# The first block's first product in plain float32, its weights in three loads, seven warm-ups

## The chip, the cores and the metric

The kernel runs on one core of a Trainium2 chip. The metric is the device time of one execution in microseconds; the median of three runs is given. A core has engines that run side by side and wait for each other through semaphores: TensorE (PE in the profile, its weight loads PEld) multiplies matrices, VectorE (DVE), ScalarE (ACT) and GpSimd (POOL) work on tiles, and SyncE (SP) starts most of the DMA transfers.

## The reference, cut to what matters

Two branches are computed from `q` (2048 x 512) and mixed by a gate per row. Branch `a` is a short causal convolution of `k` with four taps, times `v`, then a causal convolution as long as the sequence (by Fourier transforms), plus a direct term, times `q`. Branch `b` is a two-layer network on `q`.

```python
g = sigmoid((x * gate_w).sum(-1, keepdims=True))
k_shift = sum(k_pad[:, t:t + S, :] * shift_k[:, ks - 1 - t] for t in range(ks))
kv = k_shift * v
y = irfft(rfft(kv, 2 * S) * rfft(ssm_k, 2 * S))[:S] + kv * ssm_D
a = q * y
b = relu(x @ w1) @ w2          # x: 2048 x 512, w1: 512 x 1792, w2: 1792 x 512
out = g * a + (1 - g) * b
```

The change touches the first numbers of `x @ w1`, and the load of the taps `shift_k`.

## The kernel before, in words

**Products in three.** Both layers of branch `b` are computed almost to float32 from operands that are rounded to a shorter format (float32r). An operand is split into a rounded part `h` and the rest `l`: `split` (L288 to L302) has ACT (or DVE) copy the loaded tile into `h`, and DVE subtracts `h` from the tile to give `l`. A product of a weight block and a tile of `x` is then three matmuls added in PSUM: `h` by `h`, `h` by `l`, `l` by `h`.

**Tiles.** `x` transposed comes as four chunks of 512 rows of the sequence, each in four slices `k` of 128 along the 512 channels; such a slice is a tile of 128 x 512, 256 KB. `w1` gives 14 blocks `f` of 128 output columns. A block of the first layer for one chunk is thus four slices of three matmuls, 12 in all, into one bank of PSUM. The 14 blocks are worked in two halves (`ERAS`), and within each half chunk after chunk: first layer, then second layer.

**The first block of work.** For the first chunk the blocks f = 0 to 3 (`G` = 4) are done together, slice by slice, so that work can begin with the first slice of everything. Their weights come slice-wise in tiles of 128 x 512 (`wf`). `mlp1_first` writes the order out by hand: for slice 0 first `h`-`h` and `h`-`l` of blocks 0 and 1, then of blocks 2 and 3, then `l`-`h` of all four; for slices 1 to 3 each of the three terms for all four blocks. That is 12 matmuls a slice, 48 in all, on line L362.

**Its loads.** The weights of slice 0 are loaded by ACT's queue in two halves of 256 columns (L329), each followed by ACT's rounding copy of that half (L334), and DVE's rest of the whole tile (L337). The other slices of weights and all of `x` are loaded by SP's queue in the order x0, x1, w1, x2, w2, x3, w3 (L288); ACT rounds them at L299, except x0, which DVE rounds; DVE takes the rests at L302.

**Warm-ups.** Before all that PE does nine matmuls on a constant tile (`warm`, L753, `WARM` = 9).

**The planner.** Operations are not issued as written but as `Plan.order` decides: a simulation with costs written by hand (`MM` = 0.227 for a matmul, `TILES` = 0.865 for a visit of small tiled matmuls, `ISSUE` = 0.47 for starting a DMA, `DMA_RATE`), ranks, buffers that must be free, and lists that hold an order (`fifo`). The three lists `turnACT`, `turnDVE` and `turnPE` fix the order of the first block's work on these engines. A matmul planned before `PE_COLD` = 4.4 counts twice its cost. The result is one fixed order per engine. The rest of the work, the convolutions among it, is fitted in by rank: stage 1 of the Fourier transforms (L459) and the later stages (L575, L652, L727) are plain float32 matmuls in tiles of 32 or 64 rows and columns.

**The taps.** `conv_x(0)` loads the four rows of taps, repeated over the 128 partitions, in two loads of two rows each from SP's queue (L497), 512 KB written by each. DVE multiplies by them at L512 and L515.

Of the kernel before, what the change touches and what calls it, by code (L numbers as in the profile page):

```python
# [13 lines left out]
S, D, DFF = 2048, 512, 1792  # L14
P = 128
# [51 lines left out]
def _flat(r):  # L67
    for x in r if isinstance(r, tuple) else (r,):
        yield from _flat(x) if isinstance(x, tuple) else (x,)


class Plan:
# [5 lines left out]
    def add(self, eng, dur, rank, fn, deps=(), take=(), give=(), dma=0, fifo=(), tiles=False, port=False, alt=None, pair=0, soon=False, ends=False):  # L78
        rank = tuple(_flat(rank))
        op = dict(tiles=tiles, alt=alt, port=port or eng == "POOL" and not dma, eng=eng, dur=dur, rank=rank, fn=fn, take=tuple(take), give=tuple(give), dma=dma, fifo=tuple(fifo),  # L80
                  pair=pair, soon=soon, ends=ends or soon, wait=0, next=[], asked=0.0, n=len(self.ops), rest=(), member=False)
        op["fn"] = fn if alt is None else lambda: fn(op["eng"])
        for d in deps:
            if d is not None:
                d["next"].append(op)
                op["wait"] += 1
        for q in fifo:
            self.turn.setdefault(q, []).append(op["n"])
        self.ops.append(op)
        return op  # L90
# [144 lines left out]
def act_time(n, psum=False):  # L235
    return n * 0.000833 + (0.05 if psum else 0.093)


def dve_time(n):
    return n * 0.001042 + 0.12  # L240


MM = 0.227
TILES = 0.865
SWITCH = 0.19
ROW = P * D * 4


def build(tc, wf, xp, qn, kn, vn, hn, dn, sh, gw, w1, w2, cs1, ccf, cci, cib, out):
    nc = tc.nc  # L250
# [6 lines left out]
    mp = pool("mp")  # L257
# [11 lines left out]
    add = plan.add  # L269
    T = {}  # L270
    cpool = [None, None]

    def tile_of(key, tag, w=D, dt=F32, bufs=None, rows=P, p=None):
        nm = tag + "_" + "_".join(map(str, key[1:] if len(key) > 1 else key))
        T[key] = (p or cpool[0]).tile([rows, w], dt, tag=tag, bufs=bufs or room.get(tag, 1), name=nm)
        return T[key]

    def bank(key, tag="cv"):
        T[key] = pm.tile([P, D], F32, tag=tag, bufs=room0[tag], name="_".join(map(str, key)))
        return T[key]  # L280

    room0 = dict(room)
    rows = lambda x: x.rearrange("p (r d) -> p r d", d=D)
    mm = nc.tensor.matmul


    def loaded(key, src, rank, p=None, tag="raw", deps=(), eng="SP"):
        go = lambda: (nc.sync if eng == "SP" else nc.scalar).dma_start(tile_of(key, tag, p=p), src)  # L288
        return add(eng, ISSUE, rank, go, deps, take=[tag], dma=ROW, fifo=[tag])

    xdone, wdone, xhigh = {}, {}, {}
    ERAS = [range(0, NF // 2), range(NF // 2, NF)]
    CHUNKS = [list(range(NCHUNK)), list(range(NCHUNK))[::-1]]

# [11 lines left out]

    def load_x(era, c, k, rank):
        key = ("x", era, c, k)
        ld = loaded(key, xp[c, k], rank - 3, mp)
        xhigh[era, c, k], xdone[era, c, k] = split(key, "x", (0, rank), ld, 4, mp, ["x"], ["raw"], "DVE" if rank == -1000 else "ACT", rank < -900)  # L310

    def load_w(i, f, rank):
# [4 lines left out]
    def load_first(k, rank):  # L317
        key = ("w", 0, "g", k)
        if k:
            ld = loaded(key, wf[k], rank, tag="ev")  # L320
            wdone["gh", k], wdone["g", k] = split(key, "w0", -2000, ld, WB, wp, ["w1"], ["ev"], "ACT", True)
            return
        hi, lo = ("w", "h", 0, "g", 0), ("w", "l", 0, "g", 0)
        z = [slice(0, 2 * P), slice(2 * P, D)]

        def ld(i):
            if not i:
                tile_of(key, "ev")
            nc.scalar.dma_start(T[key][:, z[i]], wf[0][:, z[i]])  # L329

        def h(i):
            if not i:
                tile_of(hi, "w0h", dt=F32R, bufs=WB, p=wp)
            nc.scalar.copy(T[hi][:, z[i]], T[key][:, z[i]])  # L334

        def l():
            nc.vector.tensor_tensor(tile_of(lo, "w0l", dt=F32R, bufs=WB, p=wp), T[key], T[hi].bitcast(F32), op=OP.subtract)  # L337

        for i in range(2):
            e = add("ACT", ISSUE, -3000 + i, lambda i=i: ld(i), (), [] if i else ["ev"], dma=ROW // 2, fifo=[] if i else ["ev"])  # L340
            f = ["w1", "turnACT"] if not i else ["turnACT"]
            wdone["gh", 0, i] = add("ACT", act_time(D // 2), -2000, lambda i=i: h(i), [e] if not i else [e, wdone["gh", 0, 0]], f[:-1], fifo=f)
        wdone["g", 0] = add("DVE", dve_time(D), -2000, l, [wdone["gh", 0, 1]], (), ["ev"], port=True, fifo=["turnDVE"])

    def part(h, f, k):
        if f < G:
# [7 lines left out]
    def mlp1_first():  # L354
        prev = [None] * G
        terms = (("h", "h"), ("h", "l"), ("l", "h"))
        first = [(0, n, f) for m in range(2) for n in range(2) for f in (2 * m, 2 * m + 1)] + [(0, 2, f) for f in range(G)]
        for i, (k, n, f) in enumerate(first + [(k, n, f) for k in range(1, 4) for n in range(3) for f in range(G)]):
            def go(k=k, f=f, n=n):
                a, b = terms[n]  # L360
                ps = bank(("m1", 0, 0, f), "cv") if k == n == 0 else T["m1", 0, 0, f]
                mm(ps, part(a, f, k), T["x", b, 0, 0, k], start=k == n == 0, stop=k == 3 and n == 2)  # L362

            prev[f] = add("PE", MM, (1, -9, i), go, [((wdone["gh", k] if k else wdone["gh", 0, f // 2]), xhigh[0, 0, k]), (xdone[0, 0, k],), (wdone["g", k],)][n] + (prev[f],),
                          ["cv"] if k == n == 0 else (), fifo=["turnPE"])
        for f in range(G):
            mlp1_out(0, 0, f, prev[f])
# [121 lines left out]
    sload = [None]  # L489

    def conv_x(c):
        rank = (1, X0 + XP * c)
        if c == 0:
            def taps():
                tile_of(("sht",), "sht", 4 * D)
                for j in (2, 0):
                    nc.sync.dma_start(rows(T["sht",])[:, j:j + 2], sh[j:j + 2].partition_broadcast(P))  # L497

            sload[0] = add("SP", 2 * ISSUE, rank[1] - 3, taps, dma=4 * ROW)
        for m in range(c + 2 if c else 0, c + 3):  # L500
            kload[m] = load_in(("k", m), kn[:, 2 * m:2 * m + 2], rank[1])
        vload[c] = load_in(("v", c), vn[:, R * c:R * c + R], rank[1])
        w = lambda j, n: rows(T["sht",])[:, j:j + 1].to_broadcast([P, n, D])
        prev = None
        for j in (3, 2, 1, 0):
            dst = ("acc", c) if j == 3 else ("tmp", c, j)
            tag = dst[0]

            def mul(j=j, dst=dst, part=None):
                o = T[dst] if part == 1 else tile_of(dst, dst[0], R * D)  # L510
                if part is None:
                    nc.vector.tensor_tensor(rows(o), rows(T["k", c + (j == 1)]), w(j, 2), op=OP.mult)  # L512
                else:
                    z, u = slice(part * D, (part + 1) * D), slice((1 - part) * D, (2 - part) * D)
                    nc.vector.tensor_tensor(o[:, z], T["k", c + (j == 0) + part][:, u], T["sht",][:, j * D:(j + 1) * D], op=OP.mult)  # L515

            def plus(dst=dst):
                nc.vector.tensor_tensor(T["acc", c], T["acc", c], T[dst], op=OP.add)  # L518

            if j % 2:  # L520
                e = add("DVE", dve_time(R * D), rank, mul, [kload[c + (j == 1)], sload[0]], [tag], fifo=[tag], port=True)
            else:
                e = add("DVE", dve_time(D), rank, lambda f=mul: f(part=0), [kload[c + (j == 0)], sload[0]], [tag], fifo=[tag], port=True)
                e = add("DVE", dve_time(D), rank, lambda f=mul: f(part=1), [kload[c + (j == 0) + 1], e], port=True)
            if j != 3:
                e = add("DVE", dve_time(R * D), rank, plus, [e, prev], (), ["tmp"] + (["in"] if j == 0 else []), port=True)
            prev = e
        e = add("DVE", dve_time(R * D), rank, lambda: nc.vector.tensor_tensor(T["acc", c], T["acc", c], T["v", c], op=OP.mult),
                [prev, vload[c]], (), ["in"], port=True)
        return ("x", ("acc", c), e, ["acc"], rank)  # L530
# [218 lines left out]
    def warm():  # L749
        ps = bank(("warm",))  # L750
        one = nc.const_aps.tensor(1.0, (P, D), mybir.dt.bfloat16)
        for _ in range(WARM):
            mm(ps, one[:, :P], one, start=True, stop=True)  # L753

    w = add("PE", WARM * 2 * MM / 2, (-3,), warm, (), ["cv"], ["cv"])
    for k in range(4):
# [61 lines left out]
PATIENCE = 0.5  # L818
BEHIND = 2
G = 4  # L820
WARM = 9
DMA_AHEAD = 2.0
DMA_RATE = 300000.0
DMA_LAG = [0.575, 0.8]
# [4 lines left out]
ISSUE = 0.47  # L829
# [61 lines left out]
```

## Time and profile before

| | before |
|---|---|
| median of three runs (lowest to highest) | 385.71 us (385.69 to 385.95) |
| the profiled execution's own time | 385.97 us |
| its span, first to last instruction | 384.2 us |
| granted TensorE clock, mean | 0.999 |
| PE busy / weight loads | 379.8 us / 273.8 us |
| DVE / ACT / POOL busy | 266.7 / 128.8 / 91.5 us |
| moved by DMA | 92.51 MB, 241 GB/s |

In a row of the timeline the first number is the start in microseconds of the span, the second how long the row lasts (several instructions of one kind are merged, with their count behind an x), then engine, line, operation and tiles, and in brackets how long the engine was idle before and what ended that. A q behind an engine's name means its sequencer, which also starts DMAs. In a list of waits a row gives who waited for whom, the microseconds in total, how many times, and the longest. A row of stretches gives for each engine its busy microseconds and its instructions, then the granted clock, the mean busy share of the 16 DMA engines and the GB/s moved. A row of DMA issues gives the queue, the count, the size and the median microseconds from issue to landing. Durations of matmul rows overlap: the next can stream while the one before drains, so the pace is read from the starts.

### The profile page before, as it was taken

To read this page: it belongs to the slowest core of one execution; us is meant where nothing else is said; L and a number is where in the kernel's file an instruction comes from. 1 tells how busy PE (TensorE), PEld (TensorE's weight loads), DVE (VectorE), ACT (ScalarE), POOL (GpSimd) and SP (SyncE) were. 2 spreads that over 40 slices of the span, in tenths; PEclk is the share of its full clock that TensorE was granted. 3 is DMA by queue.
4 is the path that set the end of the run, shared out by engine and by line. 5 is a ranking of instruction groups with operands and counts; after the bars stand their busy time and mean duration, and the time that the engine had idled before them with its cause. 6 is when DMAs were issued, how large, how long until landed. Compare 5 with 4: busy or idle time off the path is not lost.

```text
span 384.2 us, 6567 instructions
## 1 busy us (share of the span) xinstructions
PE 379.8 (99%) x2505; PEld 273.8 (71%) x2505; DVE 266.7 (69%) x356; ACT 128.8 (34%) x242; POOL 91.5 (24%) x77
## 2 busy tenths in 40 slices
PE   9999999999999999999999999999999999999996
PEld 5888788668877788788655765565587788688684
DVE  4698999797989028114799687897872347687691
ACT  5643524573147525533224022313400333012100
POOL 0000000000000000000199968866995001000000
PEclk9999999999999999999999999999999999999999
DMA  7997893898648763589867876686460798399331
GB/s 274 368 317 255 298 351 113 293 333 323 208 121 330 295 234 109 185 296 275 285 203 238 307 265 227 241 308 232 139 204 3 241 342 320 120 325 357 117 124 56
DMA packets 43474, 92.51 MB, mean 241 GB/s; under 512 B 4625, under 2 KB 7201, under 8 KB 43442
## 3 DMA queue, kind: packets, MB, share of 16 engines
q1 hardware_dynamic: 43090, 91.77, 68.8%
q8 instruction: 20, 0.33, 0.4%
q10 hardware_dynamic: 288, 0.26, 0.2%
q14 instruction: 12, 0.10, 0.1%
q0 software_dynamic: 64, 0.05, 0.0%
HBM read 61.66 MB, written 30.41 MB: 240 GB/s over the span
## 4 chain that ended last, share of the span: by engine, by line
PE 99%; DVE 0%; DVEq 0%; issue 0%
PE m L406 14%; PE m L407 13%; PE m L408 13%; PE m L376 13%; PE m L377 12%; PE m L378 12%; PE iv L652 4%; PE f_h L575 4%; PE f_x L575 4%; PE m L362 3%; PE s1x L459 2%; PE s1h L459 2%; PE cy L727 2%; PE warm L753 1%; DVE o L677 0%; DVEq L887 0%
## 5 line engine op out<-in xcount | busy, mean ns | idle before, releaser
L623 POOL TENSOR_TENSOR p<-p,ha 128x512 f32<-128x512 f32 x32 | 41.1, 1308 | 202.2 <-DVE ha L617 201.6
L406 PE MATMUL m<-w1h_h,hh 128*128 128x512 f32 x224 | 88.7, 396 | 0.0
L407 PE MATMUL m<-w1l_l,hh 128*128 128x512 f32 x224 | 87.3, 390 | 0.0
L408 PE MATMUL m<-w1h_h,hl 128*128 128x512 f32 x224 | 87.2, 389 | 0.0
L389 ACT ACTIVATE hh<-m 128x512 fp32r<-128x512 f32 x56 | 33.1, 598 | 126.4 <-PE m L378 122.1
L392 DVE SCALAR_TENSOR_TENSOR hl<-m,hh 128x512 fp32r<-128x512 f32 x56 | 38.3, 688 | 44.5 <-ACT hh L389 44.3
L376 PE MATMUL m<-xh_h,w0h_h 128*128 128x512 f32 x160 | 63.0, 394 | 0.0
L377 PE MATMUL m<-xl_l,w0h_h 128*128 128x512 f32 x160 | 62.3, 390 | 0.0
L378 PE MATMUL m<-xh_h,w0l_l 128*128 128x512 f32 x160 | 62.3, 389 | 0.0
L406 PEld LDWEIGHTS m<-w1h_h,hh 128*128 128x128 f32 x224 | 42.0, 188 | 19.1 <-ACT ev L464 6.5
L408 PEld LDWEIGHTS m<-w1h_h,hl 128*128 128x128 f32 x224 | 42.0, 188 | 9.0
L407 PEld LDWEIGHTS m<-w1l_l,hh 128*128 128x128 f32 x224 | 42.1, 188 | 8.3
L376 PEld LDWEIGHTS m<-xh_h,w0h_h 128*128 128x128 f32 x160 | 30.0, 188 | 11.1 <-issue 4.2
L378 PEld LDWEIGHTS m<-xh_h,w0l_l 128*128 128x128 f32 x160 | 30.0, 188 | 6.4
L377 PEld LDWEIGHTS m<-xl_l,w0h_h 128*128 128x128 f32 x160 | 30.0, 188 | 6.0
L518 DVE TENSOR_TENSOR acc<-acc,tmp 128x1024 f32<-128x1024 f32 x24 | 29.3, 1222 | 0.6
L302 DVE TENSOR_TENSOR w1l_l<-raw,w1h_h 128x512 fp32r<-128x512 f32 x14 | 9.4, 686 | 17.7 <-ACT w1h_h L299 17.7
L662 ACT COPY bv<-iv 128x512 f32<-128x512 f32 x16 | 8.7, 589 | 37.1 <-PE iv L652 31.9
L515 DVE TENSOR_TENSOR tmp<-in,sht_sht 128x512 f32<-128x512 f32 x32 | 20.8, 685 | 0.1
L623 POOL TENSOR_TENSOR p<-p,qa 128x512 f32<-128x512 f32 x16 | 20.7, 1317 | 0.0
L617 DVE TENSOR_TENSOR ha<-f_x,ha 128x1024 f32<-128x1024 f32 x16 | 19.5, 1221 | 1.3 <-DVE qb L617 0.5
L623 POOL TENSOR_TENSOR p<-p,qb 128x512 f32<-128x512 f32 x16 | 20.3, 1290 | 0.0
(72 smaller groups left out, 468.1 us busy)
## 6 DMA issues: line engine op xcount, KB each, us to landing
sa<-ev SPq DMA_DIRECT2D x64, 256.0 KB, 3.0
sb<-bv SPq DMA_DIRECT2D x32, 256.0 KB, 3.4
br<-sb SPq DMA_DIRECT2D x16, 512.0 KB, 6.8
raw<-xp SPq DMA_DIRECT2D x28, 256.0 KB, 4.2
raw<-w SPq DMA_DIRECT2D x24, 256.0 KB, 3.8
r_x<-sa SPq DMA_DIRECT2D x12, 512.0 KB, 5.1
in<-kn SPq DMA_DIRECT2D x10, 512.0 KB, 5.0
r_h<-sa SPq DMA_DIRECT2D x10, 512.0 KB, 6.3
```

The lines of the kernel that those rows point to most:

```text
L376: mm(ps, part("h", f, k), T["x", "h", xe, c, k], start=k == 0, stop=False)
L377: mm(ps, part("h", f, k), T["x", "l", xe, c, k], start=False, stop=False)
L378: mm(ps, part("l", f, k), T["x", "h", xe, c, k], start=False, stop=k == 3)
L389: nc.scalar.activation(tile_of(("hh", era, c, f), "hh", dt=F32R, p=mp, bufs=HB), T["m1", era, c, f], AF.Relu)
L392: nc.vector.scalar_tensor_tensor(tile_of(("hl", era, c, f), "hl", dt=F32R, p=mp, bufs=HB), T["m1", era, c, f], 0.0, T["hh", era, c, f].bit ...
L406: mm(ps, T["hh", era, c, f][:, z], T["w", "h", 1, f], start=f == fs[0], stop=False)
L407: mm(ps, T["hh", era, c, f][:, z], T["w", "l", 1, f], start=False, stop=False)
L408: mm(ps, T["hl", era, c, f][:, z], T["w", "h", 1, f], start=False, stop=f == fs[-1])
L515: nc.vector.tensor_tensor(o[:, z], T["k", c + (j == 0) + part][:, u], T["sht",][:, j * D:(j + 1) * D], op=OP.mult)
L518: nc.vector.tensor_tensor(T["acc", c], T["acc", c], T[dst], op=OP.add)
L575: mm(ps[b][32 * j:32 * j + 32, :], T[k("cf")][at, 64 * j + 32 * o:64 * j + 32 * o + 32], T[k("r", t, j // 2)][at, (j % 2) * D:(j % 2 + 1) ...
L623: nc.gpsimd.tensor_tensor(planes("p", dst, n), planes("p", dst, n), planes(src, u, n), op=OP.add if sign > 0 else OP.subtract)
```

## The change

- Block 0 of slice 0 is no longer three matmuls of split operands. It is one matmul in plain float32, straight from the loaded tiles of weights and `x`; the matmuls that come after it in slice 0 are those of blocks 1, 2 and 3, nine in all.
- The first weights come in three loads, of 128, 128 and 256 columns, with a rounding copy for each. The plain product waits for the first load (`wdone["load", 0]`) and for the load of x0 (`xload`). The whole tile is still rounded and its rest taken; later chunks use it.
- The taps come in one load of four rows.
- `WARM` is 7 and not 9.

```diff
-    xdone, wdone, xhigh = {}, {}, {}
+    xdone, wdone, xhigh, xload = {}, {}, {}, {}
...
-        ld = loaded(key, xp[c, k], rank - 3, mp)
+        ld = xload[era, c, k] = loaded(key, xp[c, k], rank - 3, mp)
...
-        z = [slice(0, 2 * P), slice(2 * P, D)]
+        z = [slice(0, P), slice(P, 2 * P), slice(2 * P, D)]
...
-        for i in range(2):
-            e = add("ACT", ISSUE, -3000 + i, lambda i=i: ld(i), (), [] if i else ["ev"], dma=ROW // 2, fifo=[] if i else ["ev"])
+        for i in range(3):
+            e = add("ACT", ISSUE, -3000 + i, lambda i=i: ld(i), (), [] if i else ["ev"], dma=P * 4 * (z[i].stop - z[i].start), fifo=[] if i else ["ev"])
             f = ["w1", "turnACT"] if not i else ["turnACT"]
-            wdone["gh", 0, i] = add("ACT", act_time(D // 2), -2000, lambda i=i: h(i), [e] if not i else [e, wdone["gh", 0, 0]], f[:-1], fifo=f)
-        wdone["g", 0] = add("DVE", dve_time(D), -2000, l, [wdone["gh", 0, 1]], (), ["ev"], port=True, fifo=["turnDVE"])
+            wdone["load", i] = e
+            wdone["gh", 0, i] = add("ACT", act_time(z[i].stop - z[i].start), -2000, lambda i=i: h(i), [e] if not i else [e, wdone["gh", 0, i - 1]], f[:-1], fifo=f)
+        wdone["g", 0] = add("DVE", dve_time(D), -2000, l, [wdone["gh", 0, 2]], (), ["ev"], port=True, fifo=["turnDVE"])
...
-        first = [(0, n, f) for m in range(2) for n in range(2) for f in (2 * m, 2 * m + 1)] + [(0, 2, f) for f in range(G)]
+        first = [(0, n, f) for m in range(2) for n in range(2) for f in (2 * m, 2 * m + 1) if f] + [(0, 2, f) for f in range(1, G)]
+
+        def plain():
+
+            mm(bank(("m1", 0, 0, 0), "cv"), T["w", 0, "g", 0][:, :P], T["x", 0, 0, 0], start=True, stop=False)
+
+        prev[0] = add("PE", 4 * MM, (1, -9, -1), plain, [wdone["load", 0], xload[0, 0, 0]], ["cv"], fifo=["turnPE"])
...
-            prev[f] = add("PE", MM, (1, -9, i), go, [((wdone["gh", k] if k else wdone["gh", 0, f // 2]), xhigh[0, 0, k]), (xdone[0, 0, k],), (wdone["g", k],)][n] + (prev[f],),
+            prev[f] = add("PE", MM, (1, -9, i), go, [((wdone["gh", k] if k else wdone["gh", 0, min(f, 2)]), xhigh[0, 0, k]), (xdone[0, 0, k],), (wdone["g", k],)][n] + (prev[f],),
...
-                for j in (2, 0):
-                    nc.sync.dma_start(rows(T["sht",])[:, j:j + 2], sh[j:j + 2].partition_broadcast(P))
+                nc.sync.dma_start(rows(T["sht",]), sh.partition_broadcast(P))
 
-            sload[0] = add("SP", 2 * ISSUE, rank[1] - 3, taps, dma=4 * ROW)
+            sload[0] = add("SP", ISSUE, rank[1] - 3, taps, dma=4 * ROW)
...
-WARM = 9
+WARM = 7
```

## The prediction, as it stood before the result

> **What bounds the kernel now.** I read the page first, its sums and its chain of waits.
>
> ```profile
> span 384.2 us, 6567 instructions
> ...
> PE 379.8 (99%) x2505; PEld 273.8 (71%) x2505; DVE 266.7 (69%) x356; ACT 128.8 (34%) x242; POOL 91.5 (24%) x77
> ...
> PE 99%; DVE 0%; DVEq 0%; issue 0%
> PE m L406 14%; PE m L407 13%; PE m L408 13%; PE m L376 13%; PE m L377 12%; PE m L378 12%; PE iv L652 4%; PE f_h L575 4%; PE f_x L575 4%; PE m L362 3%; PE s1x L459 2%; PE s1h L459 2%; PE cy L727 2%; PE warm L753 1%; DVE o L677 0%; DVEq L887 0%
> ```
>
> The chain that ended last lies on PE for 99% of the span. A busy PE is not proof of a full PE, because a matmul's end is modelled, so next I asked for the waits of PE's weight loads after 7 us, where a wait must show (the five longest of those that name another engine, and the one in the first block):
>
> ```profile
> PEld m L406 <- ACT ev L464: 6.5, 8, 0.8
> ...
> PEld f_h L575 <- DVE hl L392: 1.6, 2, 0.8
> PEld f_h L575 <- ACT bv L662: 1.2, 4, 0.3
> PEld m L376 <- ACT bv L662: 0.8, 1, 0.8
> PEld f_x L575 <- ACT bv L662: 0.6, 2, 0.3
> ...
> PEld m L362 <- ACT w0h_h_g L299: 0.3, 1, 0.3
> ```
>
> Nearly all of these stand at the borders between whole-array products and the small tiled ones. The chain in order of time shows such a border:
>
> ```profile
> 82.82 1.04 PE s1x L459 x16
> 83.86 0.86 PE s1h L459 x16
> 84.72 0.43 PE m L406
> 85.15 0.23 PE m L407
> ```
>
> Whole-array products go at 0.23 us each; one visit to the tiled form costs about 0.18 extra going in (1.04 against 0.86) and 0.20 coming out (0.43 against 0.23), 0.4 in all. Away from the borders I found no wait. So the end is set by when the first block gets into its stride, plus a row of PE work in which nothing is idle. Hence the start, in the timeline of single engines:
>
> ```profile
> 0.78 3.95 PE L753 MATMUL warm<-const-bfloat16-1.0 128*128 128x512 bf16 x9 [0.78 <-PEq L884]
> ...
> 6.46 1.08 PE L362 MATMUL m<-xh_h,w0l_l_g 128*128 128x512 f32 x4
> 7.43 1.19 PE L362 MATMUL m<-xh_h,w0h_h_g 128*128 128x512 f32 x4
> ```
>
> and in narrow stretches of it, so that single products come apart:
>
> ```profile
> 3.29 1.44 PE L753 MATMUL warm<-const-bfloat16-1.0 128*128 128x512 bf16 x3
> 3.72 1.01 PE L753 MATMUL warm<-const-bfloat16-1.0 128*128 128x512 bf16 x2
> 4.14 0.59 PE L753 MATMUL warm<-const-bfloat16-1.0 128*128 128x512 bf16 x1
> 4.31 0.66 PE L362 MATMUL m<-xh_h,w0h_h_g 128*128 128x512 f32 x1
> 4.80 0.40 PE L362 MATMUL m<-xh_h,w0h_h_g 128*128 128x512 f32 x1
> 5.04 0.40 PE L362 MATMUL m<-xl_l,w0h_h_g 128*128 128x512 f32 x1
> ```
>
> The warm-ups start 0.43 apart, so the seventh (start 3.29) is through at 3.72 and the ninth at 4.57. The first real product is recorded from 4.31, but it can stream only behind the ninth warm-up, 4.57 to 4.80, and that is already the full pace of 0.23. So TensorE doubles its pace somewhere between the ninth warm-up's start and 4.57. The group of four from 6.46 steps (1.08 - 0.39) / 3 = 0.23, so its last streams from 7.15 to 7.38. That is the end of the first slice (k=0), and the second slice opens at 7.43. What it waited for, and what the other engines did:
>
> ```profile
> 7.43 0.76 PEld L362 LDWEIGHTS m<-xh_h,w0h_h_g 128*128 128x128 f32 x4 [0.33 <-ACT w0h_h_g L299]
> ...
> 3.85 0.41 ACT L334 CAST w0h_h_g<-ev_g 128x256 fp32r<-128x256 f32 x1 [0.91 <-DMA ev_g<-wf]
> 4.85 0.41 ACT L334 CAST w0h_h_g<-ev_g 128x256 fp32r<-128x256 f32 x1 [0.59 <-DMA ev_g<-wf]
> 5.16 0.61 ACT L299 CAST xh_h<-raw 128x512 fp32r<-128x512 f32 x1
> 6.75 0.62 ACT L299 CAST w0h_h_g<-ev_g 128x512 fp32r<-128x512 f32 x1 [0.98 <-DMA ev_g<-wf]
> ...
> 3.68 0.43 DVE L299 CAST xh_h<-raw 128x512 fp32r<-128x512 f32 x1 [3.68 <-DMA raw<-xp]
> 4.14 0.69 DVE L302 TENSOR_TENSOR xl_l<-raw,xh_h 128x512 fp32r<-128x512 f32 x1
> 5.29 0.69 DVE L337 TENSOR_TENSOR w0l_l_g<-ev_g,w0h_h_g 128x512 fp32r<-128x512 f32 x1 [0.46 <-ACT w0h_h_g L334]
> ```
>
> This is the reading on which all rests. Two things meet at about 7.4: PE is through with slice 0 at 7.38, and the rounded weights of slice 1 are ready at 6.75 + 0.62 = 7.37. ACT had stood idle for 0.98 before that cast, for a DMA. Whoever makes slice 0 shorter on PE meets the DMA at once.
>
> **The change, part by part.** *Fewer warm-ups.* Two less free PE 4.57 - 3.72 = 0.85 earlier. *Plain product.* It removes three products of 0.23 (f=0 of slice 0) and adds one of plain float32. The trace has plain float32 only in tiles:
>
> ```profile
> L459 PE MATMUL s1h<-in,s1c_s1t x128: 587/587/638, 38.3 to 159.5; 32*64 32x512 f32 x128
> ```
>
> Sixteen of them, eight tiles in two passes each, fill the array once and take 0.86 in the chain (the s1h row). A full-array plain product should thus take about 0.86 at full pace (lower bound: the 0.23 of one rounded product; upper bound: 1.70, at half pace throughout: four passes of 0.43). I take 0.86 and correct for the pace. It needs no cast, only the loads: x at 3.68, when DVE starts on it, and the first 128 weight columns, of which 256 came by 3.85. So it starts at about 3.75, with hardly a hole behind the warm-ups. Up to 4.57 it runs at half pace: 0.82 us do 0.41 of work; the rest, 0.45, ends at 5.02. Nine products of 0.23 to 0.24 follow: 7.15. Before, the twelve end at 7.38. **PE gains 0.23**, the whole of it in this slice, before any wait.
>
> *Three loads.* ACT issues one DMA more, ahead of its table load:
>
> ```profile
> 0.74 0.89 ACTq L329 DMA_DIRECT2D ev_g<-wf  x2
> 1.66 1.28 ACT L334 ACT_TABLE_LOAD   x1 [1.66 <-PEq L884]
> ```
>
> One issue costs 0.89 / 2 = 0.45, so the table load ends at 3.4 and not 2.94, still ahead of the first data. The last half of the weights is issued 0.45 later. It landed at 4.85; between 4.85 and 5.3 now. Cast 0.41, so at worst 5.71, and PE wants f=2 at 5.02 + 2 x 0.235 = 5.49: at worst 0.22 of hole, which brings slice 0 back to 7.37. DVE's rest of the weights then runs 5.75 to 6.44, and PE wants it at 6.44 or later. Two small casts in place of one (0.41) cost ACT some 0.1 of fixed time, inside its idle 0.98. So this part costs nothing by itself; without that idle time it would cost 0.1.
>
> *The wait that takes its place.* Slice 1's weights are the third load of SP's queue:
>
> ```profile
> 0.74 0.85 SPq L288 DMA_DIRECT2D raw<-xp  x2
> 1.65 0.42 SPq L288 DMA_DIRECT2D ev_g<-wf  x1
> ...
> ev_g<-wf SPq DMA_DIRECT2D x1, 256.0 KB, 5.1
> ...
> 4.00:4.50 0.50, 0.50 (x3) 0.19 (x1) 0.47 (x2) 0.26 (x1) 0.00 (x0) 1.00 1.10 359
> 6.00:6.50 0.50, 0.50 (x4) 0.41 (x3) 0.50 (x1) 0.00 (x0) 0.00 (x0) 1.00 0.98 377
> ```
>
> Issued at 1.65, landed 5.1 later, with the DMA engines full (share 1.10 and 0.98). Neither its place nor the bytes ahead of it change: x for two slices and the first weights, 256 KB each, are the same in two pieces or in three. So it lands at 6.75 again, ACT ends at 7.37, PE opens slice 1 at 7.43, and the 0.23 won becomes a longer wait, 7.15 to 7.43. The bounds are as wide as I can reason: at 360 GB/s a piece of 128 KB is 0.36 us, so if that piece moves out of this load's way or into it, it lands 0.36 earlier or later. I take zero, because all these bytes are queued well before 6.
>
> [...]
>
> *Taps.* One load for two. An issue less on SP:
>
> ```profile
> 5.23 1.00 SPq L497 DMA_DIRECT2D sht_sht<-sh  x2
> 6.79 4.93 SPq L288 DMA_DIRECT2D raw<-w  x4
> ```
>
> That is 0.5 at 5.7, behind which SP stood until 6.79 anyway (6.23 to 6.79 idle). The taps' first reader starts at 20.5, so even a load that lands a microsecond later harms nobody.
>
> *The planner.* The order of all later work is planned again, with these durations. By hand: a product before 4.4 is counted twice over, so the plan has warm-ups to 3.18, the plain product 3.6 to 5.4, slice 0 to 7.4 against 7.2 before. The planned transfers up to slice 1's weights come some 0.2 later too. Both shift together, so I expect the same order or one changed in places that nobody waits for. Price if not, below.
>
> **Sum.** -0.23 on PE, +0.23 of new wait: 0 at slice 1 (bounds -0.38, rival 1, to +0.36), 0 after it. The profiled execution took 385.97 with its span of 384.2, the median of the runs shown is 385.71, inside their spread of 0.26; I carry the difference over to the median and say 385.7.
>
> **Rivals.** *(1) The weights of slice 1 come sooner*, and the win on PE is seen. For it: the last 128 KB of ACT's queue start later and leave the engines to SP's queue for a while. Against it: the total ahead is equal. PE then opens slice 1 at 7.15 and not 7.43, and with no exposed weight load: the group of four that opened slice 1 took 1.19 where an undisturbed one takes 1.08. Together 0.28 + 0.11, time 385.3.
>
> *(2) The replanned order breaks something.* One pair of tiled visits taken apart costs 0.4, one missed operand of a DVE pass 0.69: 386.1 to 386.8. For it: PE is so full that any difference can only be a loss. Against it: the shift is 0.2, and the shift is common to PE and transfers.
>
> *(3) TensorE stays at half pace* (the slower side). Seven warm-ups end at 3.72, before the pace doubled; the rest must be bridged by a product that waits for two DMAs. If the hole puts off the doubling past slice 0, the plain product takes 1.71 from 3.75 and nine more 0.43 each: 9.3 in place of 7.43, +1.9, time 387.6. It decides from an opening later than about 5.1. For it: x came at 3.68, only just ahead of 3.72. Against it: a hole of 0.05 to 0.15 in four microseconds of work. [...]
>
> *(4) It doesn't do what it says*: the loads land later than x, the plain product starts at 4.2, slice 0 ends at 7.4: again 385.7.
>
> **Chances.** Forecast (hidden) with (4) 0.63; (1) 0.18; (2) 0.13; (3) 0.06. The forecast's own range is 385.4 to 386.0. To leave out no more than 2 in 10 the range takes in (1) and the nearer part of (2): 385.1 to 386.4. A measurement of this kernel tells 0.2% from nothing, 0.77 us. A win of that size would need slice 1 to open at 6.66, and PE cannot be there before about 7.1: 0.03. Slower by as much: (3), and half of (2): 0.12. Same: 0.85.
>
> **What would show it.** The plain product as two records from about 3.75 and the next product at about 5.0; slice 0 ending near 7.15; then a weight load that waits some 0.3 to 0.5 for ACT's cast, with DMA as that cast's releaser at about 6.75; the same visits of tiled products afterwards, eight and their kind. Wrong it is if slice 1 opens before 7.2 or after 7.8, or if matmuls go at 0.43 after 5.1, or if a wait longer than 0.8 shows in PE's weight loads later.

## The result, and the profile after

The changed kernel takes 386.95 us (median of 12 runs, 386.44 to 389.59), the kernel before 385.82 (12 runs). The ratio is 1.0035, with a 95% interval from 1.0026 to 1.0044: slower by about 1.1 us, outside the range on record and on the side that was given 0.12.

The page of the kernel after:

```profile
span 384.9 us, 6565 instructions
...
PE 379.6 (99%) x2502; PEld 273.1 (71%) x2502; DVE 262.5 (68%) x351; ACT 128.3 (33%) x243; POOL 97.3 (25%) x82
...
PE 97%; DMA 1%; ACTq 0%; DVE 0%; ACT 0%; DVEq 0%; issue 0%
```

PE has lost 2% of the chain, and a DMA has come in. The chain in order of time says which (start, length, what):

```profile
1.18 0.45 ACTq L329
1.63 0.03 issue
1.66 4.60 DMA ev_g<-wf
6.26 0.02 issue
6.28 0.41 ACT w0h_h_g L334
6.70 0.04 issue
6.74 10.08 PE m L369 x43
```

It is the third of the three loads. Issued at 1.66, it lands 4.60 later. PE and ACT in the timeline of the kernel after:

```profile
0.78 3.14 PE L759 MATMUL warm<-const-bfloat16-1.0 128*128 128x512 bf16 x7 [0.78 <-PEq L890]
3.89 1.25 PE L362 MATMUL m<-raw,ev_g 128*128 128x512 f32 x2
5.09 0.50 PE L369 MATMUL m<-xh_h,w0h_h_g 128*128 128x512 f32 x1
5.43 0.39 PE L369 MATMUL m<-xl_l,w0h_h_g 128*128 128x512 f32 x1
6.74 0.74 PE L369 MATMUL m<-xh_h,w0h_h_g 128*128 128x512 f32 x2 [0.91 <-ACT w0h_h_g L334]
...
8.48 1.09 PE L369 MATMUL m<-xh_h,w0h_h_g 128*128 128x512 f32 x4
...
3.87 0.30 ACT L334 CAST w0h_h_g<-ev_g 128x128 fp32r<-128x128 f32 x1 [0.44 <-DMA ev_g<-wf]
4.74 0.30 ACT L334 CAST w0h_h_g<-ev_g 128x128 fp32r<-128x128 f32 x1 [0.58 <-DMA ev_g<-wf]
6.28 0.41 ACT L334 CAST w0h_h_g<-ev_g 128x256 fp32r<-128x256 f32 x1 [1.24 <-DMA ev_g<-wf]
7.11 0.62 ACT L299 CAST w0h_h_g<-ev_g 128x512 fp32r<-128x512 f32 x1
```

The plain product goes nearly as predicted: from 3.89, two records, the next product at 5.09, right behind ACT's cast of the second piece (4.74 + 0.30). Then PE has two products to do, until 5.66, and stands idle for more than a microsecond, because blocks 2 and 3 need the last 256 columns. At 6.74 it goes on without a break, and slice 1 opens at 8.48 in place of 7.43. Its own weights were rounded at 7.73: they are no longer what comes last.

Behind the first block nothing is lost. The weight loads' waits at the borders between whole-array and tiled products are nearly the same in number and length (the row of ACT's copies again, and the new wait of the first block):

```profile
PEld m L413 <- ACT ev L471: 6.5, 8, 0.8
...
PEld m L369 <- ACT w0h_h_g L334: 2.1, 2, 1.4
```

The first tiled visit comes 0.92 later than before, those from 127 on 0.70 later; 0.22 was made up in one visit near 121 us, which had been longer in the kernel before. So the span is 0.7 longer in the two profiled executions (384.9 against 384.2), and that is not all of the 1.1. The rest lies outside the span: the time less its span was 1.77 in the profiled execution of before (385.97 - 384.2) and 2.02 in that of after (386.92 - 384.9). Over the runs this part has a median of 1.78 before (27 runs, none over 1.92), and 2.0 after (12 runs, up to 2.95). The median spans are 384.1 and 384.95. Two things are to be explained, then: 0.85 in the span and 0.2 behind it.

### The profile page after: what moved, and what is told of

Its sections match the earlier page's. It is cut to its first block, busy times and chain, and to the rows that moved or that the text cites. A ratio compares the mean times of both kernels' runs of the same rounds, so it can differ in the third digit from the quotient of the medians.

```text
span 384.9 us, 6565 instructions
## 1 busy us (share of the span) xinstructions
PE 379.6 (99%) x2502; PEld 273.1 (71%) x2502; DVE 262.5 (68%) x351; ACT 128.3 (33%) x243; POOL 97.3 (25%) x82
## 4 chain that ended last, share of the span: by engine, by line
PE 97%; DMA 1%; ACTq 0%; DVE 0%; ACT 0%; DVEq 0%; issue 0%
PE m L413 14%; PE m L415 13%; PE m L414 13%; PE m L383 13%; PE m L385 12%; PE m L384 12%; PE iv L658 4%; PE f_h L581 4%; PE f_x L581 4%; PE m L369 3%; PE s1x L466 2%; PE cy L733 2%; PE s1h L466 2%; DMA ev_g<-wf 1%; ACTq L329 0%; DVE o L683 0%
## 5 line engine op out<-in xcount | busy, mean ns | idle before, releaser
L302 POOL TENSOR_TENSOR xl_l<-raw,xh_h 128x512 fp32r<-128x512 f32 x12 | 15.5, 1325 | 22.7 <-ACT xh_h L299 22.7
```

Of the source, the lines that this page charges most:

```text
L302: (nc.gpsimd if eng == "POOL" else nc.vector).tensor_tensor(tile_of(lo, tag + "l", dt=F32R, bufs=bufs, p=p), T[key], T[hi].bitcast(F32), o ...
```

## The experiments

"Ready" is the start of ACT's cast of the last columns, in the one profiled execution of each kernel. "Outside" is time less span, median and largest. Each ratio is to the runs of before that were made alongside: 12 with a median of 385.82 for the changed kernel, 33 with 385.94 for the last four rows, and 27 with 385.85 for the others.

| kernel | time, median (runs) | ratio to before, 95% | span | outside | ready |
|---|---|---|---|---|---|
| before | 385.85 (27) | | 384.1 | 1.78, 1.92 | 4.85 |
| changed | 386.95 (12) | 1.0026 to 1.0044 | 384.95 | 2.00, 2.95 | 6.28 |
| two_loads | 386.14 (10) | 0.9992 to 1.0011 | 383.95 | 1.87, 2.81 | 4.96 |
| late_second | 386.55 (10) | 1.0007 to 1.0027 | 384.35 | 2.05, 2.78 | 4.94 |
| three_only | 387.19 (6) | 1.0021 to 1.0045 | 385.4 | 1.78, 1.81 | 6.47 |
| warm9 | 386.64 (10) | 1.0010 to 1.0028 | 384.75 | 1.78, 1.89 | 5.93 |
| late_second3 | 388.69 (4) | 1.0053 to 1.0106 | 386.6 | 1.91, 2.13 | 6.84 |
| halves7 | 386.44 (11) | 1.0003 to 1.0021 | 384.4 | 2.06, 3.01 | 5.00 |
| before_warm7 | 385.86 (11) | 0.9995 to 1.0019 | 384.0 | 1.78, 2.42 | 5.04 |
| plain_only | 386.14 (11) | 0.9998 to 1.0016 | 384.3 | 1.75, 1.90 | 4.95 |
| w1_held | 386.63 (10) | 1.0001 to 1.0024 | 384.25 | 1.94, 2.89 | 5.73 |
| halves7_short2 | 385.69 (11) | 0.9985 to 1.0003 | 383.8 | 1.79, 1.90 | 5.00 |
| after_short2 | 386.62 (11) | 1.0008 to 1.0027 | 384.8 | 1.77, 1.89 | 7.28 |
| taps_two | 386.78 (10) | 1.0019 to 1.0037 | 385.0 | 1.76, 2.40 | 5.95 |

### Is it the third load, and why is it late?

My first theory was one of turns: the two queues are served a load at a time in turn, so that ACT's third load goes behind SP's third.

**two_loads.** The columns of the third load go with the second; casts and planned order stay.

```diff
         def ld(i):
             if not i:
                 tile_of(key, "ev")
-            nc.scalar.dma_start(T[key][:, z[i]], wf[0][:, z[i]])
+            if i < 2:
+                u = slice(z[i].start, D if i else P)
+                nc.scalar.dma_start(T[key][:, u], wf[0][:, u])
```

> The changed kernel with the first weights in two loads (128 and 384 columns) and the same three casts, in the same planned order. Theory T (turns): ACT's queue and SP's queue are served a load at a time in turn, so ACT's third load goes behind SP's third (slice 1's weights, 256 KB); with two loads the last 256 columns come with the second turn, ready for ACT at 4.8 to 5.2 and not 6.28, PE waits nowhere for them, slice 1 opens at 7.4 to 7.6, and the time is that of before within 0.3 us (about 1 us under the changed kernel). Rival P (the plain product and its lack of cover): the cost is PE's, not the load's; slice 1 opens at 8.3 or later, time 386.7 to 387.1.

The load of 384 columns is ready at 4.96, slice 1 opens at 7.48, the median span falls by 1.0. So what the span had lost is the third load's, and the plain product is not to blame: the rival P falls. The size is less certain than the cause: undoing the three loads in another way (halves7, below) takes 0.55 off the span, and putting them into the kernel before (next) adds 1.3.

**three_only.** The three loads and casts put into the kernel before, with nothing else.

```diff
-        z = [slice(0, 2 * P), slice(2 * P, D)]
+        z = [slice(0, P), slice(P, 2 * P), slice(2 * P, D)]
...
-        for i in range(2):
+        for i in range(3):
```

> The kernel before with the first weights in three loads and casts, nothing else of the change. Theory T: the third load is ready for ACT at 6.2 to 6.4; blocks 2 and 3 of slice 0 wait for it, PE stands idle about 1.1 us, slice 1 opens at 8.4 to 8.7, time 386.6 to 387.1. Rival P: the three loads are hidden, slice 1 opens at 7.4 to 7.6, time as before within 0.2 us.

The three loads alone do it, and more: ready at 6.47, span 385.4, time 387.19 and so 0.1 above the range. PE in its timeline:

```profile
5.44 0.63 PE L362 MATMUL m<-xl_l,w0h_h_g 128*128 128x512 f32 x2
...
6.93 0.74 PE L362 MATMUL m<-xh_h,w0h_h_g 128*128 128x512 f32 x2 [0.86 <-ACT w0h_h_g L334]
```

**late_second** and **late_second3** are two_loads with the second load held back. GpSimd fills the columns before, once in the first and three times in the second; ACT's load has to wait for it.

```diff
                 tile_of(key, "ev")
+                for _ in range(3):
+                    nc.gpsimd.memset(T[key][:, P:], 0.0)
```

> As two_loads, but the second load is held back on ACT by about 0.4 us: GpSimd first fills the columns that it will write, and the load waits for that. It is then issued when the changed kernel's third load was (about 1.65). Theory T: its turn is still the second, it is ready for ACT by 5.3, and the time is that of two_loads within 0.2 us. Rival I (late issue): a load issued at 1.65 is served behind all that was issued before, whatever its number; ready for ACT at 6.1 to 6.4, slice 1 at 8.4, time 386.7 to 387.1.

The filling took 0.42 and was over at 1.16, when ACT had just become free: the load was not delayed (issue 1.19), and the run says nothing on turns. Its time, 386.55, lies 0.4 above two_loads and in neither range; what its profiled execution lost is told further below.

> two_loads with the second load held back until about 2.0: GpSimd fills the columns three times first (0.42 each, from 0.74), and ACT waits for it. (Filled once, in late_second, it was done at 1.16 and delayed nothing.) The load is then issued after SP's third load (1.65), which is slice 1's weights. Theory T (turns): it still takes ACT's second turn, beside or right after the second slice of x, ready for ACT at 5.0 to 5.4; slice 1's weights then come behind it. Rival I (late issue): what was issued first is served first; it comes behind slice 1's weights, ready at 6.2 or later.

Here the load is issued at 2.14. The DMA issues of three narrow stretches of late_second3 (queue, count, size, microseconds from issue to landing), from 1.3, from 1.7 and from 2.2:

```profile
raw<-xp SPq DMA_DIRECT2D x1, 256.0 KB, 3.3
...
ev_g<-wf SPq DMA_DIRECT2D x1, 256.0 KB, 3.6
...
raw<-xp SPq DMA_DIRECT2D x1, 256.0 KB, 4.9
ev_g<-wf ACTq DMA_DIRECT2D x1, 192.0 KB, 4.7
```

With the issues at 1.18, 1.65, 2.12 and 2.14 they land at 4.5, 5.3, 7.0 and 6.8. ACT's second load does not land with the second slice of x, as a second turn would have it; it lands with what was issued beside it, behind slice 1's weights, which had been issued 0.5 before, though its own queue had only one load ahead of it. My theory of turns falls as I had stated it, and the rival holds here: **what was issued half a microsecond before, on either queue, came first** (5.3 against 6.8). Whether the engines would have shared out between two loads that were both waiting, this run does not show: from 4.0 to 4.5 all 92 packets are of SP's queue, but whether ACT's load was already waiting at the DMA engines then, 2 us after its issue, the trace does not tell.

Then the kernel after is read in the same way; its issues in the stretches from 1.3 and from 1.7:

```profile
raw<-xp SPq DMA_DIRECT2D x1, 256.0 KB, 3.4
...
ev_g<-wf SPq DMA_DIRECT2D x1, 256.0 KB, 4.4
ev_g<-wf ACTq DMA_DIRECT2D x1, 128.0 KB, 4.6
```

The third piece is issued at 1.66, a hundredth behind slice 1's weights at 1.65. What the two queues moved from 4.5 to 5.25 (q1 is SP's, q10 is ACT's; packets, MB, share):

```profile
q1 hardware_dynamic: 102, 0.18, 67.0%
q10 hardware_dynamic: 124, 0.12, 44.5%
```

Of the piece's 0.13 MB nearly all goes out here, side by side with slice 1's weights and not behind them. It shares the DMA engines with these 256 KB, after all that was issued before. The second half of before was issued at 1.18, in a draw with the second slice of x, and shared with that one (from 3.4 to 4.4, 119 packets of q1 and 142 of q10): half a microsecond earlier in the line.

**w1_held.** The counter-test: the changed kernel, with slice 1's weights held back on SP until the third piece is out.

```diff
+        def go():
+            t = tile_of(key, tag, p=p)
+            if key == ("w", 0, "g", 1):
+                for _ in range(3):
+                    nc.gpsimd.memset(t[:, P:], 0.0)
+            (nc.sync if eng == "SP" else nc.scalar).dma_start(t, src)
```

> The changed kernel, with SP's third load (slice 1's weights) held back from 1.65 to about 2.05 by GpSimd filling its tile three times first. Theory O (order of issue, formed after late_second3): both queues' loads are served in the order in which they were issued. Then ACT's third load (1.66) goes ahead, is ready for ACT at 4.9 to 5.4 and not 6.28, PE waits for it by 0.3 at most, and slice 1's weights land at 6.2 to 6.9; slice 1 opens at 7.2 to 7.9, time 385.9 to 386.5. Theory T (a turn for each load): it still waits for SP's third load whenever that comes, ready at 6.2 or later, time 386.9 or more.

Issues in the stretches from 1.7 and from 2.15:

```profile
ev_g<-wf ACTq DMA_DIRECT2D x1, 128.0 KB, 4.0
...
ev_g<-wf SPq DMA_DIRECT2D x1, 256.0 KB, 3.9
```

Issued at 1.66 and 2.13, they land at 5.7 and 6.1: the order is turned round, and the median span falls from 384.95 to 384.25. The landing is later than I expected (5.7, not 4.9 to 5.4), and the time, 386.63, lies 0.1 above the range of theory O, so order of issue is not the whole of it; this piece has landed between 5.9 and 7.3 in the profiles of the five kernels that have it as the third, with the same issues. The latest, 7.3 in after_short2 (below), comes from one laggard: the loads of ACT's queue end with sixteen packets of 4 B each (48 for the three in the trace of the kernel after), and fifteen of this one's are through by 5.3, as all sixteen are in warm9 (below), but the last only at 6.9. What makes a part lag, I have not shown.

### The time behind the span

**warm9**, **before_warm7** and **plain_only** take the change apart in another direction: the changed kernel with `WARM = 9`, the kernel before with `WARM = 7`, and the kernel before with the plain product alone (nine warm-ups, two halves, taps in two loads).

> The changed kernel with nine warm-ups. Theory T: PE waits for the third load at 6.3 to 6.7 anyway, so two warm-ups more (0.85) push the plain product to 4.57 and fill idle time; slice 1 opens where it does with seven (8.4 to 8.5), time as the changed kernel's within 0.2 us. Rival W (too few warm-ups): with nine TensorE has its full pace earlier and the time falls by 0.3 us or more.

> The kernel before with seven warm-ups and nothing else. PE is free at 3.72 and waits for the first cast until about 4.3; slice 0 ends about where it did if the clock opens at 4.5, later by up to 0.7 where it opens later. Theory T: time as before within 0.3 us. Rival W (too few warm-ups): the hole from 3.72 to 4.3 puts off the opening of the clock or adds time outside the span, time 386.2 or more.

> The kernel before with the plain product alone (first weights in two halves, nine warm-ups, taps in two loads). Theory T: the plain product starts behind the ninth warm-up at 4.57 and is through at about 5.45; nine products of 0.23 follow: slice 0 ends at 7.5, slice 1 opens at 7.5 to 7.6; time as before to 0.2 us over it (385.8 to 386.1). Rival P: 386.3 or more.

warm9 came out 0.3 under the changed kernel, as its rival W had it, 0.2 of it in the span and 0.2 outside. In the span, warm-ups and plain product count 0.2 at most, by the medians: 384.75 with nine against 384.95; 384.0 with seven in the kernel before against 384.1; 384.3 with the plain product alone, whose time of 386.14 lies between the ranges of its theory and of rival P. But the column "outside" splits by one thing only. With nine warm-ups it is 1.7 to 1.9 in every run of four kernels. With seven it scatters, with largest values of 2.1 to 3.0, though the median can stay where it was (1.78 in before_warm7). The page's queue of instruction fetches (q8, blocks of 16 KB) tells where they differ. In the kernel before one such block falls between 374 and 377. In before_warm7 and in halves7 (next) there is none from 372 to 383.5; there is one in the stretch from 383.7, behind the last instruction. This row is halves7's, from 384 on:

```profile
DMA packets 1, 0.02 MB, mean 5 GB/s; under 512 B 0, under 2 KB 0, under 8 KB 0
...
q8 instruction: 1, 0.02, 2.0%
```

So theory F: the program of PE is four instructions shorter (two weight loads, two matmuls), and its last block of instructions (I take these blocks for PE's, the one program that the warm-ups shorten) is no longer asked for while the work goes on, but when it is over.

**halves7** undoes the three loads alone (`range(2)`, halves as before, all else as changed). **halves7_short2** and **after_short2** add two very short warm-ups to halves7 and to the changed kernel: as many instructions as with nine, while PE is free about as early as with seven.

```diff
         for _ in range(WARM):
             mm(ps, one[:, :P], one, start=True, stop=True)
+        for _ in range(2):
+            mm(ps[:, :32], one[:, :P], one[:, :32], start=True, stop=True)
```

> The changed kernel with the three loads undone: two of 256 columns, one cast each; plain product, seven warm-ups and one taps load kept. Theory T: no load takes a third turn on ACT; the plain product starts at 3.9 as in the changed kernel, since the first load lands no later for being larger; the second block's first product does not wait for the second load; slice 0 is through at 7.1 to 7.2 where TensorE's clock opens by 4.6, slice 1 opens with its weights at 7.0 to 7.5; time 385.4 to 386.0, no slower than before. Rival P: the plain product costs something by itself, time 386.3 or more.

> halves7 with two very short warm-ups more (32 columns), so that PE's program has as many instructions as with nine while it is free as early as with seven. Theory F (instruction fetch): with seven, PE's program is four instructions shorter, its last block of instructions is fetched after the last instruction of the span, and that time lies open outside the span. With the two short ones the fetch falls at about 375 again, time outside the span is 1.7 to 1.9 in every run (it was 1.76 to 3.01), and the time falls by 0.2 to 0.4 against halves7, to 386.0 to 386.2, at or under before. Rival C (clock): the time outside belongs to the early end of the warm-ups and stays scattered up to 2.5 and more.

> The changed kernel with the two short warm-ups. Theory F: time outside the span 1.7 to 1.9 in every run, spans as in the changed kernel (384.7 to 385.2), time 386.4 to 386.8, some 0.2 to 0.3 under it. Rival C: as the changed kernel, 386.9 with a scatter outside the span.

halves7 missed its range on the slow side and came out where rival P had it (386.44), half of the miss outside the span. With the short warm-ups the scatter is gone: 22 runs of 22 lie between 1.72 and 1.90, and a block is fetched between 372 and 384 again. That is what F expected, and the rivals C and P fall. One number is not what F expected: halves7_short2 is 0.75 under halves7 and not 0.2 to 0.4, and 0.6 of that is in the span (383.8 against 384.4), which F does not explain. halves7_short2 is the best version of all: 385.69, 1.3 under the changed kernel; against the kernel before the ratio is 0.9994 with an interval of 0.9985 to 1.0003, no difference that can be told.

So two short products more in the program make the difference outside the span. That the late fetch is the cause is likely, not shown. None of the eight profiles with seven warm-ups and no short ones has a block near 375. In four it stands behind the last instruction: 1.7 to 1.8 behind it in before_warm7, halves7 and w1_held, with 2.3 to 2.6 outside, and 0.5 behind it in taps_two (next), with only 1.7 outside. In the other four, the changed kernel's among them, the trace has no block of this queue after 362, and 1.8 to 2.1 outside.

**taps_two.** The changed kernel with the taps in two loads, as before.

> The changed kernel with the taps in two loads, as before. Theories O and F: nothing waits for the taps, slice 0 is as in the changed kernel, and PE's program has the same length: time as the changed kernel's within 0.3 us. Rival: the single load holds up the raw weights behind it; with two loads the time falls by 0.3 or more.

Span 385.0 against 384.95: the taps count nothing in the span. Outside, it scatters less (1.76, though up to 2.4); why, I don't know.

### What late_second and late_second3 lost besides

late_second has its weights in time and still opens slice 1 at 8.03. PE in its timeline:

```profile
3.92 2.07 PE L365 MATMUL m<-raw,ev_g 128*128 128x512 f32 x2
5.29 1.06 PE L372 MATMUL m<-xh_h,w0h_h_g 128*128 128x512 f32 x1
6.18 0.39 PE L372 MATMUL m<-xl_l,w0h_h_g 128*128 128x512 f32 x1
```

The plain product takes 2.07 and not 1.25, and the product behind it 1.06: in this execution TensorE came to full pace (0.23 from product to product; before it the warm-ups step by 0.43) near 6.1. In that of before it did by 4.57, and in that of the changed kernel, with the same seven warm-ups from 0.78, at 4.18 (where the trace's record of the granted clock begins, at 1.00). late_second3 shows the reverse. PE waits for its late load from about 5.2 to 7.19, and then the columns of stretches (PEclk is the third number from the end) read:

```profile
5.50:7.00 1.50, 0.00 (x0) 0.00 (x0) 0.00 (x0) 0.16 (x1) 0.00 (x0) 1.00 1.06 392
7.00:8.00 1.00, 0.81 (x2) 0.71 (x3) 0.52 (x1) 1.00 (x4) 0.00 (x0) 0.51 1.05 399
9.00:10.00 1.00, 1.00 (x4) 0.74 (x3) 1.00 (x3) 1.00 (x4) 0.00 (x0) 0.50 0.91 385
10.50:11.50 1.00, 1.00 (x6) 0.82 (x5) 1.00 (x3) 0.59 (x2) 0.00 (x0) 1.00 0.92 375
```

Behind a hole of 2 us the full pace was gone, from 7.0 to some point between 10 and 10.5. A hole alone is not enough, though. after_short2 waits for its late third piece nearly as long and goes on at full pace (the groups of two below take 0.56 and 0.46 from start to start, where two products at half pace would take 0.86):

```profile
7.74 0.73 PE L369 MATMUL m<-xh_h,w0h_h_g 128*128 128x512 f32 x2 [1.87 <-ACT w0h_h_g L334]
8.30 0.62 PE L369 MATMUL m<-xl_l,w0h_h_g 128*128 128x512 f32 x2
8.76 0.85 PE L369 MATMUL m<-xh_h,w0l_l_g 128*128 128x512 f32 x3
```

What separates the two is not shown. One of the changed kernel's 12 runs took 389.59 with a mean granted clock of 0.994, the figure of late_second3's profiled execution; that its hole did the same there is likely, but there is no trace of that run.

## Why the prediction was wrong

**The step that failed is "Three loads".** The prediction put the last piece's landing "between 4.85 and 5.3", 0.45 later than before, because its issue is 0.45 later, and closed with "so this part costs nothing by itself". It was ready at 6.28, and that cost the 0.85 in the span (0.55 to 1.3 by halves7, two_loads and three_only). The mis-sized term is the landing: I moved it one for one with the issue, as if a load had a duration. Here it had a place in a line. The rows for that stood in the trace of before, for the issues at 0.74 and at 1.18:

```profile
raw<-xp SPq DMA_DIRECT2D x1, 256.0 KB, 2.9
ev_g<-wf ACTq DMA_DIRECT2D x1, 128.0 KB, 3.1
...
raw<-xp SPq DMA_DIRECT2D x1, 256.0 KB, 3.5
ev_g<-wf ACTq DMA_DIRECT2D x1, 128.0 KB, 3.6
```

The one issued at 1.65 landed 5.1 later, a row that I quoted for another purpose. Whoever moves this load's issue from 1.18 to 1.66 must read off the landing of a load issued then, and from more than one execution: slice 1's weights, issued at 1.65 each time, landed 3.6 to 5.1 later in the ten profiles that tell it.

**"The wait that takes its place"** named the wrong load. I looked for what PE would meet after slice 0 and found slice 1's weights; it met its own slice's last weights first. Those of slice 1 landed sooner than before (at 6.05, 4.4 after their issue), but were rounded at 7.73 and not at 7.37, since ACT casts in a fixed order and had the late piece ahead of them. And the meeting of PE and DMA at about 7.4, "the reading on which all rests", belonged to one execution. In plain_only's profile slice 1 opens without a wait:

```profile
7.10 1.07 PE L369 MATMUL m<-xh_h,w0h_h_g 128*128 128x512 f32 x4
```

That is what rival 1 speaks of, though the medians show no gain (span 384.3 against 384.1).

**Right in mechanism, and nearly in size:** the plain product (its record from 3.89 to 5.14, where I had 3.75 to 5.02). That the end fits so well is partly luck: I had half pace until 4.57, and full pace came at 4.18; and the next product waited for a cast until 5.04 anyway. The "four passes" behind the upper bound of 1.70 were my estimate and no run shows them: the traces have the plain product as two records, 1.12 us in all in halves7_short2 and 2.07 at half pace in late_second. My assumption that a smaller first piece lands earlier, or at least no later, gave nothing: 64 KB were ready at 3.87, 128 KB before at 3.85. **Right:** the taps cost nothing in the span (taps_two); the replanned order breaks nothing (the tiled visits come in the same order, and 0.22 was even won).

**"Fewer warm-ups"** was costed at PE's free time only. In the span that holds. What I left out is that the program gets shorter, and that this reached beyond the last instruction: 0.2 at the median of the changed kernel, up to 1.2 in single runs. No rival had it, and no view of the span can show it.

**Rival 3** (half pace) was not what happened to the median. But the opening it speaks of, the start of full pace, does move: it lay by 4.57 in the profile of before and near 6.1 in late_second's. The time as predicted took the opening of one execution for a fixed one.

**The chances.** "Same" had 0.85 on the ground that all bytes ahead were equal. They were equal ahead of slice 1's weights, and not ahead of the third piece. "Slower" had 0.12, for rivals 2 and 3; what happened is neither of them, so that these 0.12 were on the right side is luck.

## What to carry to other kernels

Cost a moved or split load by what stands ahead of it in the order of issue, over the queues together, and read its landing from a load issued at that time, not from its old duration: here an issue 0.48 later (1.66 for 1.18) was a landing 1.43 later (6.28 for 4.85). The piece that was split off for an earlier start pushed the remainder back, to a place beside 256 KB that nobody needed yet. And look at the time less the span as a figure of its own: here two products of 32 columns more took its largest value from 3.01 (halves7) to 1.90 (halves7_short2).

## What the runs showed of the hardware that I had not expected

- Loads of ACT's and SP's queues went in the order of their issue where half a microsecond lay between them: in late_second3 a second load of ACT's queue issued at 2.14 landed at 6.8, beside SP's of 2.12 (7.0), and behind SP's of 1.65 (5.3). In the kernel after, two that were issued a hundredth apart (1.65 and 1.66) went out side by side (102 and 124 packets from 4.5 to 5.25).
- The last block of the queue of instruction fetches came after the last instruction in four of the profiles, 0.5 to 1.8 us behind it. In kernels of nine warm-ups, or of seven and two short ones, it came some 9 us before the end of the profiled execution, and the time outside the span was 1.7 to 1.9 in every run; with seven alone that time went up to 3.0, and no profile has a block there. That the program does this is shown by the pairs with and without two products of 32 columns; that the fetch is what lengthens the end is not, for half of the profiles with seven show no late block.
- Full pace of TensorE came at 4.18 in one profiled execution and near 6.1 in another, with the same warm-ups; behind a wait of 2 us on PE it was gone for 3 us and more in late_second3 (PEclk 0.51 from 7 to 8 and 0.50 to 10, 1.00 from 10.5), behind one of 1.87 in after_short2 it was not (two products in 0.46). What decides when it comes or goes, no run shows.
